# The first K tile of a decode kernel, loaded as two halves of columns from two queues

## The chip, the cores and the metric

The kernel runs on one core of one Trainium2 chip. The metric is device time in microseconds (us) of one execution. A core has five engines that each run their own program in order (TensorE, VectorE, ScalarE, GpSimd, SyncE), and 16 DMA engines that move data between the chip's main memory and the on-chip memory of 128 partitions. Programs wait for one another through semaphores; a DMA raises its semaphore when its data has landed.

## The reference

One decoding step of attention with a cache, mixed with a gated feed-forward block. Sizes: x has 448 values; there are 16 query heads and 8 K/V heads, each with a cache of 65536 positions by 256 values in bf16; the feed-forward width is 1792.

```python
g = sigmoid((x * gate_w).sum(-1))
q = (x @ wq).reshape(16 heads, 256)
scores = q . k / 16            # two query heads share one K/V head
a = softmax(scores) @ v        # reshaped to 4096 values
a = a @ wo
b = ((gate * (gate > 0)) * up) @ W_down    # gate = x @ W_gate, up = x @ W_up
out = g * a + (1 - g) * b
```

K and V together are 537 MB, the weights some 12 MB, and each byte is read once.

## The kernel before, in words

**Tiles.** Each of the 8 K/V heads has its 65536 positions cut into four tiles of 16384, for K and for V: 32 K tiles and 32 V tiles, of 8 MB each. A tile lies on 128 partitions with 128 positions (`U = 128`) of 256 values, 64 KB a partition, contiguous in main memory. Three ring buffers of that size hold all of the large data: buffer 0 first wq and W_down, then the gate and up weights, then V tiles, and wo at the end; buffers 1 and 2 hold K tiles in turn, and the last V tiles.

**What happens to a K tile.** VectorE transposes it in place in four pieces (`f_trans`, L529). TensorE then makes the scores in two halves, each of which waits for two of the four pieces (`f_qk`, L540: 64 matmuls a tile). VectorE takes the maximum (L703), ScalarE the exponential (L705). After the fourth tile of a head, a short chain rescales and transposes the probabilities, and TensorE multiplies them with the head's V tiles (`f_pv`, L584).

**The order of the work** is written out by hand. Every operation is given a key, a due time that the author reckons from a list of loads (`order`) with a price for each; an engine's program is its operations sorted by that key, and the waits follow from the declared dependencies. The loads are issued by SyncE, in this order: K0, wq (two DMAs, L626 and L627), K1, W_down (L675), K2, the gate and up weights (four DMAs, L640 and L642), K3, K4, V0, and from then on K and V in turn (L680 for K, L772 for V). A load that reuses a ring buffer waits on SyncE for the last reader of what lay there: K2 goes where K0 was and waits for K0's second half of scores; the gate and up weights wait for the q matmuls; V0 waits for the matmuls with W_down. The first four of the list wait for nothing.

**The opening.** ScalarE issues two small DMAs: x (key -9, L421) and gate_w (key -8, L422), each one row of 0.9 KB. In VectorE's program stand, in this order: constants; then what needs x (L478 and L479, then L488 to L494, with a small TensorE step at L485 between them, which turns x into columns); then what needs both x and gate_w (L464, L465; ScalarE's exponential at L466; L468 to L470; a small matmul at L471; L472, L475), which gives g and 1 - g; and then the four transposes of K0. TensorE makes q when wq is there (L501, 28 matmuls). After the transposes of K0 VectorE turns q (L632, which waits for ScalarE's copy of q, L630) and spreads it (L513); ScalarE copies the first head's part (L634); a small transpose at L635; then the scores of K0.

The load of a K tile and its transposes are declared so:

```python
kd = dma("sp", t, "r%d" % sl, lambda e, n=n, sl=sl: e.dma_start(ring[sl][:], k_src(n)), free(("k", n)))
tk = max(tL["k", n], last.get("free", 0))
tr = [op("dv", tk + 4.5 * w, f_trans(sl, w), [kd]) for w in range(4)]
```

`dma("sp", t, ...)` puts the DMA into SyncE's program with key `t`; `free` lists whose work must be over before the buffer is overwritten, and is empty for K0.

Of the kernel before, what the change touches and what calls it, by code (L numbers as in the profile page):

```python
# [27 lines left out]
class _Plan:  # L28
# [8 lines left out]
    def op(self, eng, key, fn, deps=(), tag=None):  # L37
        eng, cls = {"pv": ("pe", "pv"), "dx": ("dv", "dx"), "ap": ("ac", "ap")}.get(eng, (eng, eng))
        o = _Op(eng, key, fn, deps, tag=tag, cls=cls)
        self.ops.append(o)  # L40
        return o

    def dma(self, eng, key, sem, fn, deps=()):
        if sem not in self.dsem:
            self.dsem[sem] = self.es.enter_context(self.nc.semaphore("d_" + sem))
        o = _Op(eng, key, fn, deps, dma=sem)
        self.ops.append(o)
        return o
# [212 lines left out]
def bass_gated_mix__gqa_block_cached__glu_gated_reglu__decode_kernel(  # L261
# [20 lines left out]
    U = 128  # L282
# [14 lines left out]
    with es:  # L297
# [3 lines left out]
        ring = [sb("ring%d" % i, [128, U * DH], BF) for i in range(NRING)]  # L301
# [69 lines left out]
        op, dma = pl.op, pl.dma  # L371
# [23 lines left out]
        t = 3.0  # L395
# [10 lines left out]
        def place(kind, i):  # L406
            if kind == "k":
                return 1 + i % 2
            if kind == "v":
                return 1 + i % 2 if i >= NT - NTH else 0  # L410
            return {"vp": 2, "wo": 0}[kind]

        for kind, i, _ in order:
            if kind in ("k", "v") or (kind, i) in (("wo", 0), ("vp", 0)):
                r = place(kind, i)
# [101 lines left out]
        def k_src(n):  # L517
            h, t_ = divmod(n, NTH)
            return A_k_cache[0, h, :, :].rearrange("(p t u) d -> p t (u d)", t=NTH, u=U)[:, t_, :]
# [7 lines left out]
        def f_trans(sl, w):  # L527
            v = ring[sl][:, w * 8192:(w + 1) * 8192].bitcast(U32)
            return lambda e: e.transpose(v, v)  # L529
# [34 lines left out]
        def free(key):  # L564
            out_ = []
            for f in freed[key]:
                out_.append(l_[f] if isinstance(f, str) else qk[f[1], 1] if f[0] == "k" else pv[f[1]])
            return out_
# [55 lines left out]
        for kind, i, t in sorted(issue, key=lambda q: q[0] != "wq"):  # L624
# [51 lines left out]
            elif kind == "k":  # L676
                n = i
                h, t_ = divmod(n, NTH)
                sl = slot["k", n]
                kd = dma("sp", t, "r%d" % sl, lambda e, n=n, sl=sl: e.dma_start(ring[sl][:], k_src(n)), free(("k", n)))  # L680
                tk = max(tL["k", n], last.get("free", 0))
                tr = [op("dv", tk + 4.5 * w, f_trans(sl, w), [kd]) for w in range(4)]
                if n > 1:
                    tr[1].deps.append(aexp[n - 2])
                if t_ == 0:
# [82 lines left out]
            elif kind in ("v", "vp"):  # L768
                if kind == "v":
                    n, lo, hi = i, 0, U  # L770
                    sl = slot["v", n]
                    dep = dma("sp", t, "r%d" % sl, lambda e, sl=sl, n=n: e.dma_start(ring[sl][:], v_src(n)), free(("v", n)))  # L772
                else:
                    n, (lo, hi) = NT - 1, PIECES[i]
                    sl = slot["vp", 0]
# [96 lines left out]
```

## Time and profile before

| | |
|---|---|
| median of 3 runs | 1276.91 us (1276.64 to 1276.96) |
| the profiled execution | 1276.31 us |
| its span in the profile | 1274.5 us |
| busy: TensorE, VectorE, ScalarE | 355.0, 630.1, 77.9 us |
| moved by DMA | 549.13 MB, mean 431 GB/s |

The profiled execution's time is the metric of that one execution; the span is what lies between the first and last event of the profile, 1.8 us less. In the profile SP is SyncE, ACT ScalarE, DVE VectorE, PE TensorE (PEld its weight loads) and POOL GpSimd; SPq and ACTq are the DMA issues in the programs of SyncE and ScalarE. DMA queue q1 carries what SyncE issues, q10 what ScalarE issues; q8 and q14 fetch instructions. A row of the timeline gives the start, the duration, the engine and line, the operation with its output and input, and, in square brackets, how long the engine was idle before it and what ended that. K0, K1, ... are the K tiles in order, V0, V1, ... the V tiles.

### The profile page before, as it was taken

What the parts mean: (1) busy time and instruction counts of PE and PEld (TensorE: products, weight loads), DVE (VectorE), ACT (ScalarE), POOL (GpSimd) and SP (SyncE); (2) the same over time, 40 slices, a digit from 0 to 9 for tenths busy, and PEclk for the clock granted to TensorE, in tenths of its full rate; (3) what the DMA queues carried; (4) which work ended last, traced back from release to release, by engine and by line L of the source; (5) the groups of instructions that cost most, each with busy time, mean ns of one, the idle gap of its engine ahead of it and who ended that gap; (6) DMA issues with size and microseconds to landing.
All of it is one profiled execution on the core that took longest, in us unless ns stands there. A gap on an engine that the chain in (4) does not pass through costs nothing.

```text
span 1274.5 us, 10236 instructions
## 1 busy us (share of the span) xinstructions
PE 355.0 (28%) x4497; PEld 146.9 (12%) x4505; DVE 630.1 (49%) x309; ACT 77.9 (6%) x163; POOL 4.6 (0%) x23
## 2 busy tenths in 40 slices
PE   0534321132320332212223221323202242103524
PEld 0101110011110111101111110111100111001201
DVE  4777655553455633557433565336554355554300
ACT  0001100010000100001000010001000010000100
POOL 1000000000000000000000000000000000000000
PEclk9766665666655666656666656666566666566667
DMA  9999999999999999999999999999999999999998
GB/s 411 440 428 428 430 432 434 444 430 430 430 432 438 438 432 432 428 434 438 438 430 432 428 434 440 436 432 430 430 432 442 436 430 430 432 430 444 434 417 367
DMA packets 11389, 549.13 MB, mean 431 GB/s; under 512 B 1267, under 2 KB 1654, under 8 KB 2294
## 3 DMA queue, kind: packets, MB, share of 16 engines
q1 hardware_dynamic: 11378, 549.03, 99.7%
q8 instruction: 4, 0.07, 0.0%
q14 instruction: 3, 0.02, 0.0%
q10 hardware_dynamic: 4, 0.00, 0.0%
HBM read 549.03 MB, written 0.00 MB: 431 GB/s over the span
## 4 chain that ended last, share of the span: by engine, by line
DMA 81%; PE 15%; DVE 2%; ACT 1%; issue 1%; SPq 0%; ACTq 0%
DMA ring<-in_A_v_cache_dram 74%; PE O L584 13%; DMA ring<-in_A_wo_dram 3%; DMA ring<-in_A_wq_dram 2%; DMA ring<-in_A_k_cache_dram 2%; DVE ring L529 1%; PE ST L540 1%; ACT pcur L591 1%; PE O L501 1%; PE A_ps L551 0%; SPq L785 0%; PE O L653 0%; SPq L776 0%; DVE ring L660 0%; PE A_ps L653 0%
## 5 line engine op out<-in xcount | busy, mean ns | idle before, releaser
L529 DVE STREAM_TRANSPOSE ring<-ring 128x4096 uint32<-128x4096 uint32 x128 | 557.6, 4413 | 205.9 <-DMA ring<-in_A_k_cache_dram 205.9
L584 PE MATMUL O<-ring,pcur 128*4 128x512 bf16 x2048 | 179.6, 527 | 798.0 <-ACT pcur L591 789.4
L703 DVE TENSOR_REDUCE nmb<-ST 128x1 f32<-128x512 f32 x32 | 22.1, 692 | 336.6 <-PE ST L540 336.6
L584 PEld LDWEIGHTS O<-ring,pcur 128*4 128x4 bf16 x2048 | 57.3, 108 | 916.9 <-ACT pcur L591 802.1
L540 PE MATMUL ST<-ring,xcur 128*16 128x512 bf16 x2048 | 135.0, 416 | 45.5 <-DVE ring L529 44.9
L540 PEld LDWEIGHTS ST<-ring,xcur 128*16 128x16 bf16 x2048 | 61.0, 92 | 113.0 <-DVE ring L529 49.3
L705 ACT ACTIVATE P_sb<-ST,nmb 128x512 bf16<-128x512 f32 x32 | 44.5, 1392 | 360.3 <-DVE nmb L703 360.3
L591 ACT COPY pcur<-ptp 128x256 bf16<-128x256 bf16 x32 | 13.2, 414 | 740.4 <-DMA ring<-in_A_v_cache_dram 740.4
L607 DVE TENSOR_SCALAR o_sb<-O,rcm 128x256 bf16<-128x256 f32 x8 | 3.8, 479 | 60.9 <-PE O L584 60.9
L730 DVE TENSOR_TENSOR P_sb<-P_sb,hs 128x1024 bf16<-128x1024 bf16 x16 | 18.9, 1222 | 8.1 <-ACT hs L724 8.1
L735 PE MATMUL PT<-identb,P_sb 128*128 128x128 bf16 x128 | 13.8, 272 | 18.0 <-DVE P_sb L730 17.9
L501 PE MATMUL O<-ring,P_sb 128*128 128x512 bf16 x28 | 8.7, 484 | 17.4 <-DMA ring<-in_A_wq_dram 17.4
L735 PEld LDWEIGHTS PT<-identb,P_sb 128*128 128x128 bf16 x128 | 10.0, 121 | 20.3 <-DVE P_sb L730 20.3
L744 ACT COPY ptp<-PT 128x256 bf16<-128x256 bf16 x32 | 10.3, 375 | 22.7 <-PE PT L735 22.7
L705 ACT ACTIVATION_READ_ACCUMULATOR P_sb<-ST,nmb 128x1 f32 x32 | 8.3, 259 | 0.0
L501 PEld LDWEIGHTS O<-ring,P_sb 128*128 128x128 bf16 x28 | 3.2, 118 | 22.4 <-issue 20.8
L756 DVE RECIPROCAL rc<-M_ps 128x2 f32<-128x2 f32 x8 | 1.4, 171 | 7.5 <-PE M_ps L755 7.5
L719 PE MATMUL M_ps<-identf,hs 128*2 128x128 f32 x8 | 2.3, 283 | 10.0 <-DVE hs L717 10.0
L551 PE MATMUL A_ps<-ring,attnA 128*1 128x224 bf16 x64 | 4.1, 258 | 2.3 <-DMA ring<-in_A_wo_dram 2.2
L755 PE MATMUL M_ps<-hs,ones_f 128*128 128x2 f32 x16 | 4.5, 352 | 0.0
L557 PE MATMUL A_ps<-o_sb,ecur 128*128 128x32 bf16 x64 | 3.2, 191 | 3.1 <-DVE o_sb L610 3.1
L722 PE MATMUL M_ps<-mx,nselT 2*128 2x1 f32 x16 | 3.2, 268 | 3.0 <-DVE mx L721 3.0
(93 smaller groups left out, 69.4 us busy)
## 6 DMA issues: line engine op xcount, KB each, us to landing
ring<-in_A_v_cache_dram SPq DMA_DIRECT2D x1, 4096.0 KB, 21.9
ring<-in_A_wq_dram SPq DMA_DIRECT2D x1, 3072.0 KB, 28.9
ring<-in_A_v_cache_dram SPq DMA_DIRECT2D x1, 3072.0 KB, 28.9
ring<-in_B_W_down_dram SPq DMA_DIRECT2D x1, 1568.0 KB, 53.1
ring<-in_B_W_gate_dram SPq DMA_DIRECT2D x1, 1344.0 KB, 27.3
ring<-in_B_W_up_dram SPq DMA_DIRECT2D x1, 1344.0 KB, 30.2
ring<-in_A_wo_dram SPq DMA_DIRECT2D x1, 1232.0 KB, 33.3
ring<-in_A_v_cache_dram SPq DMA_DIRECT2D x1, 1024.0 KB, 30.9
```

What stands on the lines that cost most here:

```text
L501: ins = e.matmul(QN_ps, xw3[:, kt, 31 - m:159 - m], rhs, start=(kt == 0 and m == 0), stop=(kt == R3 and m == J // 4 - 1))
L529: return lambda e: e.transpose(v, v)
L540: ins = e.matmul(bank[32 * w:32 * w + 16, :], xcur[:, x0:x0 + 16], ktv[sl][:, u0:u0 + 16, c, :, r_], start=(b == 0 and c == 0 and r_ == 0) ...
L551: ins = e.matmul(A_ps[32 * g:32 * g + 1, 0:D2], lhsT, rhs[:, g * D2:(g + 1) * D2], start=start, stop=stop, skip_group_check=True, tile_pos ...
L584: ins = e.matmul(OP[32 * g:32 * g + 4, :], pcur[a % 2][:, 4 * k:4 * k + 4], ring[sl][:, k * 512:(k + 1) * 512], start=False, stop=False, s ...
L591: pc[n] = op("ap", max(tp - 5, last["tev", h] - 0.5), lambda e: e.copy(pcur[a % 2][:].rearrange("p (k i) -> p k i", i=4), ptp[:].rearrange ...
L703: smax[n] = op("dv", sx, lambda e, n=n, t_=t_: e.tensor_reduce(NM[:, t_:t_ + 1], ST[n % 2][:], AX.X, ALU.max, negate=True), [qk[n, 1], las ...
L705: aexp[n] = op("ac", sx + 1, lambda e, n=n, t_=t_: e.activation(P_sb[:, t_:2048:4], ST[n % 2][:], ACTF.Exp, bias=NM[:, t_:t_ + 1], scale=1 ...
L730: rsc = op("dv", tt, lambda e, pb=pb: e.tensor_tensor(pb, pb, X[:, 12:16].unsqueeze(1).to_broadcast([128, 256, 4]), ALU.mult), [h7, aexp[n]])
L735: ins = e.transpose(PT[rd][:, s * 128:(s + 1) * 128], P_sb[:, (rd * 8 + s) * 128:(rd * 8 + s + 1) * 128], identb[:, :])
L744: ins = e.copy(dst, src)
L755: l3 = mop("pe", T + 19, lambda e: e.matmul(LS_ps, ones_f[:, :], X[:, 6:8], start=True, stop=True), [l2, c_one], tag="l3")
```

## The change

K0 is loaded by two DMAs. SyncE's DMA, at its old place, now loads the first half of each partition's columns (positions 0 to 63 of its 128, 32 KB). ScalarE issues a DMA for the second half, with the key -10, which places it ahead of its x and gate_w loads. This DMA has a semaphore of its own (`k0`). All four transposes of K0 wait for both DMAs. The other K tiles are loaded as before, in one DMA each.

```diff
-                kd = dma("sp", t, "r%d" % sl, lambda e, n=n, sl=sl: e.dma_start(ring[sl][:], k_src(n)), free(("k", n)))
+                cols = slice(0, U * 128 if n == 0 else U * 256)
+                kd = dma("sp", t, "r%d" % sl, lambda e, n=n, sl=sl, cols=cols: e.dma_start(
+                    ring[sl][:, cols], k_src(n)[:, cols]), free(("k", n)))
+                kds = [kd]
+                if n == 0:
+                    kds.append(dma("ac", -10, "k0", lambda e, sl=sl: e.dma_start(ring[sl][:, U * 128:], k_src(0)[:, U * 128:])))
                 tk = max(tL["k", n], last.get("free", 0))
-                tr = [op("dv", tk + 4.5 * w, f_trans(sl, w), [kd]) for w in range(4)]
+                tr = [op("dv", tk + 4.5 * w, f_trans(sl, w), kds) for w in range(4)]
```

## The prediction

> **What bounds the kernel now.** I read the page first (the slices, the DMA queues, the chain that ended last), then the timeline and the chain in order of time for the first 105 us, then windows on the DMA. From the page:
>
> ```profile
> span 1274.5 us, 10236 instructions
> ...
> DMA  9999999999999999999999999999999999999998
> ...
> q1 hardware_dynamic: 11378, 549.03, 99.7%
> ...
> q10 hardware_dynamic: 4, 0.00, 0.0%
> ...
> DMA 81%; PE 15%; DVE 2%; ACT 1%; issue 1%; SPq 0%; ACTq 0%
> ```
>
> The 16 DMA engines are busy in every slice, with SyncE's queue (q1) on them 99.7% of the time. The time is 549 MB at their rate plus every moment in which they have nothing queued; compute matters only where it makes a load start late. So the question is not when the first K tile K0 lands, but whether SyncE's next issue still comes before its queue has drained. The opening, from the timeline (start, length; in brackets the engine's idle time before and who ended it):
>
> ```profile
> 0.71 0.53 ACTq L421 DMA_DIRECT2D P_sb<-in_A_x_dram  x1
> 0.72 0.41 SPq L680 DMA_DIRECT2D ring<-in_A_k_cache_dram  x1
> ...
> 1.28 0.21 ACTq L422 DMA_DIRECT2D scr<-in_gate_w_dram  x1
> ...
> 4.91 0.18 DVE L478 COPY scr<-P_sb 1x64 bf16<-1x64 bf16 x1
> ...
> 6.04 0.18 DVE L494 COPY P_sb<-xT 128x4 bf16<-128x4 bf16 x1
> ...
> 10.08 0.61 DVE L464 TENSOR_TENSOR ptp<-P_sb,scr 1x448 f32<-1x448 bf16 x1 [3.86 <-DMA scr<-in_gate_w_dram]
> ...
> 14.32 0.23 DVE L475 TENSOR_SCALAR mg<-emat,gb 128x4 f32<-128x4 bf16 x1
> 22.78 17.42 DVE L529 STREAM_TRANSPOSE ring<-ring 128x4096 uint32<-128x4096 uint32 x4 [8.23 <-DMA ring<-in_A_k_cache_dram]
> ...
> 31.45 8.68 PE L501 MATMUL O<-ring,P_sb 128*128 128x512 bf16 x28 [17.36 <-DMA ring<-in_A_wq_dram]
> ...
> 40.84 0.45 DVE L632 STREAM_TRANSPOSE scr<-ptp 128x256 uint32<-128x256 uint32 x1 [0.64 <-ACT ptp L630]
> ...
> 44.35 4.96 PE L540 MATMUL ST<-ring,xcur 128*16 128x512 bf16 x64 [0.65 <-issue]
> ...
> 49.36 0.33 SPq L680 DMA_DIRECT2D ring<-in_A_k_cache_dram  x1
> ```
>
> To be seen: ScalarE's two 0.9 KB loads (x, gate_w) land before K0. VectorE goes through the x and gate work (L478 to L475, done at 14.55), idles 8.23 us for K0, transposes it until 40.20, turns q, and TensorE's scores of K0 (44.35 on) free the ring buffer for the third K tile K2, issued at 49.36. That issue is the first that waits for compute.
>
> **How the queues share an engine.** A packet's bytes are counted at its start (columns: stretch, length, busy time of five engines, granted clock, DMA share, GB/s):
>
> ```profile
> 1.60:2.40 0.80, 0.00 (x0) 0.00 (x0) 0.62 (x5) 0.00 (x0) 0.64 (x3) 1.00 3.87 1312
> 2.40:4.60 2.20, 0.00 (x0) 0.00 (x0) 1.84 (x7) 0.00 (x0) 1.59 (x9) 1.00 0.00 0
> 4.60:5.60 1.00, 0.27 (x5) 0.22 (x5) 0.54 (x4) 0.00 (x0) 0.67 (x5) 1.00 2.42 1049
> ...
> 7.00:8.00 1.00, 0.00 (x0) 0.00 (x0) 0.00 (x0) 0.00 (x0) 0.00 (x0) 1.00 2.42 1049
> ...
> 9.40:10.40 1.00, 0.00 (x0) 0.00 (x0) 0.32 (x1) 0.00 (x0) 0.00 (x0) 1.00 2.42 1049
> ```
>
> 1049 GB/s over 1 us is 16 packets of 64 KB: every engine starts one K0 packet (one partition) each 2.42 us. gate_w, issued at 1.28, ended VectorE's wait at 10.08, just as the fourth burst began. q10 shows four packets for two loads, so each is data and a completion. The reading that fits: on an engine the two queues take turns packet by packet, and each of gate_w's two packets let 64 KB of K0 pass (one more was already under way).
>
> **The change, part by part.**
>
> *Removed and added issues.* SyncE's issue keeps its 0.41 us. ScalarE gets one of about that length (row at 0.72) ahead of its two, which move from 0.71 and 1.28 to about 1.2 and 1.7. ScalarE's next work waits for the gate_w chain: no cost in itself.
>
> *K0's arrival.* Both halves go over the same 16 engines. Packets become 32 KB and take turns, 8 and 8 per engine. At the same rate K0 is complete where it was, 22.7. Every transpose waits for both halves, so none starts earlier. Two queues could at best lift this stretch from 422 GB/s to the page's best slice, 444:
>
> ```profile
> 1.70:21.60 19.90, 0.85 (x7) 0.71 (x7) 5.55 (x23) 1.49 (x2) 3.62 (x17) 1.00 1.01 422
> 21.60:30.00 8.40, 0.00 (x0) 0.00 (x0) 7.22 (x2) 0.00 (x0) 0.00 (x0) 1.00 0.98 418
> ```
>
> 19.9 x (1 - 422/444) = 1.0 us; I take 0 (the packets run back to back already), with 1.0 as the other end.
>
> *x and gate_w, moved behind 4 MB.* They are now last in ScalarE's own queue, in order behind K0's second half. On the engine that carried gate_w, packets of 2.42 us put K0's end, landing included, at 10.08 + 5 x 2.42 = 22.2. Then come x's data, its completion, gate_w's data and its completion, each taking turns with a packet of wq (3072 KB in 128 packets, so 24.6 thousand bytes; from the 418 GB/s row above at share 0.98, 24.6 x 16 x 0.98 / 418 = 0.92 us).
>
> ```profile
> ring<-in_A_wq_dram SPq DMA_DIRECT2D x1, 3072.0 KB, 28.9
> ```
>
> Three or four of these: gate_w lands at 24.9 or 25.9; I take the middle, **25.4**. Lower end 22.8 (with K0), upper end in the rivals.
>
> *VectorE's order.* Queued behind the two waits, on an engine that works in order, are the gate chain and K0's four transposes. From gate_w's landing to the end of L475 it was 14.55 - 10.08 = 4.5 us (a ScalarE exponential with its table load and a small matmul among it), formerly inside the 8.23 us of idle. That cover is now gone: the transposes start at 25.4 + 4.5 = 29.9 instead of 22.78 and end at 47.35 instead of 40.20. The q matmuls need x only at 31.45 (x lands two turns earlier, its own chain takes 6.2 - 4.9 = 1.3 us), so they end at 40.1 as before, and the copy at L630 that L632 waited for, 0.64 us, now hides behind the transposes: L632 starts at 47.4 against 40.84, **+6.5 us**.
>
> *Scores of K0.* From L632 to K2's issue were 49.36 - 40.84 = 8.52 us, of which 4.99 the 64 matmuls. They ran half at each clock:
>
> ```profile
> 44.40:46.70 2.30, 2.30 (x24) 0.79 (x28) 0.00 (x0) 0.00 (x0) 0.00 (x0) 0.50 1.05 456
> 46.75:49.20 2.45, 2.45 (x44) 1.08 (x36) 0.00 (x0) 0.00 (x0) 0.00 (x0) 1.00 1.02 435
> ```
>
> and a half of a later tile's scores, from the timeline, all of it at 0.50:
>
> ```profile
> 84.09 3.59 PE L540 MATMUL ST<-ring,xcur 128*16 128x512 bf16 x32 [10.89 <-DVE ring L529]
> ```
>
> All at half clock the 64 would take 2 x 3.59 = 7.2, all at full clock 3.6. TensorE will have been idle 10 us instead of 4, so it starts at half clock again; I take 5.4. The Trainium skill ("TensorE: Matmul & The Clock Gate", Part 1) says the activity window is free-running and of about 3.4 us, so the clock may rise up to two windows late; that agrees with a rise 2.4 us into these matmuls, and by it the term would lie between 5.4 and 7.2, the time between my forecast and 1.8 us above it. K2's issue: 49.36 + 6.5 + 0.4 = **56.3**.
>
> *When the queue drains.* K0, wq, K1 and W_down are all issued in the first microseconds. K0's time from issue to landing, on an empty queue, and K2's in the chain (start, length):
>
> ```profile
> DMA to landing us min/median/max: 22.0/22.0/22.0
> ```
>
> ```profile
> 49.36 25.87 DMA ring<-in_A_k_cache_dram
> ...
> 104.28 36.72 DMA ring<-in_A_v_cache_dram
> ```
>
> The DMA around the point where K2 takes over, and the instruction fetches between 46 and 58:
>
> ```profile
> 53.20:54.10 0.90, 0.00 (x0) 0.00 (x0) 0.90 (x1) 0.00 (x0) 0.00 (x0) 0.70 2.64 1104
> 54.10:55.40 1.30, 0.00 (x0) 0.00 (x0) 1.30 (x1) 0.00 (x0) 0.00 (x0) 0.50 0.30 120
> 55.40:56.40 1.00, 0.00 (x0) 0.00 (x0) 1.00 (x1) 0.00 (x0) 0.00 (x0) 0.50 2.12 918
> ```
>
> ```profile
> q8 instruction: 2, 0.03, 1.1%
> ```
>
> The burst from 53.2 is K2's first packets on most engines: there the old queue ends, and K2, issued 3.8 us earlier, was ready. At 56.3 + 1.1 (K0's first burst lies 0.9 to 1.7 after its issue) it is not: those engines stand idle for about 4 us, **the first hole in the DMA stream**. K2's landing was 49.36 + 25.87 = 75.2; from an empty queue it is 56.3 + 22.0 = 78.3, or +3.1. But 75.2 holds a lag that K0's 22.0 doesn't: K2's eight packets from 53.2 to 54.1 on, 19.4 us of them and 0.3 to land (K0: its eighth burst ends at 21.5 to 22.5), would be done at 72.9 to 73.8, so some engines ran 1.4 to 2.3 late, those whose K2 burst comes only at 55.4. I put that down to the instruction fetches (q8). Fetches that fall into the hole cost nothing, later ones do. Bounds: all of the lag gone, +3.1; all kept, +3.1 + 1.8 = 4.9. I take two thirds kept, **+4.3**.
>
> *What is late next.* Again from the timeline, and the load that follows K2 in the queue:
>
> ```profile
> 52.13 17.42 DVE L529 STREAM_TRANSPOSE ring<-ring 128x4096 uint32<-128x4096 uint32 x4 [2.07 <-DMA ring<-in_A_k_cache_dram]
> ...
> 73.25 0.33 SPq L680 DMA_DIRECT2D ring<-in_A_k_cache_dram  x1
> ```
>
> ```profile
> ring<-in_B_W_gate_dram SPq DMA_DIRECT2D x1, 1344.0 KB, 27.3
> ```
>
> K1's transposes start after K0's scores, near 57.0 instead of 52.13, so K3's issue moves by 4.9 to about 78. Behind K2, done near 79, lie the gate and up weights (over 2.7 MB, 6 us or more): hidden. V0 (at 104.28) takes 36.7 to land against 22.0 on an empty queue, so it has some 15 us in hand. No later hole opens, none closes, and no idle DMA time exists to absorb this one. The sum against the profiled execution (1276.31, span 1274.5): 1276.31 + 4.3 = 1280.6. The median of the runs lies 0.6 above that execution, so as a median **1281.2**.
>
> **Rivals.**
>
> *Turns of whole transfers.* If an engine finished a transfer's share before it changes queue, x would wait for wq (8 x 0.92 = 7.3 us) and gate_w also for wq's tail (512 KB, 1.3 us): gate_w at 22.2 + 8.6 = 30.8, 5.4 later than mine, **1286.6**. Against it: gate_w had landed by 10.08, in the middle of K0. The Trainium skill ("DMA: Bandwidth & Descriptors", Queues, rings and completion order) speaks for it: an engine drains a packet of typically 9 to 17 descriptors from one queue before it switches, which is one load's share here. The trace disagrees, by that 10.08. 8%.
>
> *ScalarE's queue first (not slower).* Should the engines serve K0's second half ahead of the first, it ends near 12 and gate_w near 14; the 4.5 us chain fits in the idle time before 22.78, nothing moves: **1276.9**. It decides at a landing of about 21.7: then K2's issue is 2.8 us later, at 52.2, and its packets just meet the queue's end at 53.3. For it: x, issued 0.01 us before K0, was served at once. Against it: gate_w was made to wait 8.8 us. 9%.
>
> *Starved.* If ScalarE's half waited for SyncE's backlog, it would land near 52, K2's issue would be some 33 us late: about **1307**. The four q10 packets, served in the midst of q1, speak against it. 2%.
>
> *A better rate.* Two queues at 444 GB/s save 1.0 us and the 4.3 shrink to 3.3: **1280.2**, still slower; no mechanism in the trace takes off 2.6 us.
>
> **How the numbers follow.** Measurement can tell about 0.2%, 2.6 us: faster is below 1274.4, slower above 1279.5. The forecast has 79% (the better rate in it); its own range adds the ends (gate_w 24.9 to 25.9, scores 4.6 to 6.5, lag none to all): 1278.5 to 1283.5, and some 6 of the 79 lie under 1279.5. Transfers whole 8%, ScalarE first 9%, starved 2%; 2% is left for a gain that I see no mechanism for. Faster 2%, same 9 + 6 = 15%, slower 83%. All ends of the terms at once, scores at 3.6 and 7.2 among them, give 1277.7 to 1284.1; toward the whole transfers I go to 1285.5. Range: 1277.7 to 1285.5.
>
> **What would show it.** Right: VectorE's idle ahead of L478 or L464 ends after 23; the first L529 starts near 30, not 22.8; L632 near 47.4 follows it with no wait for ScalarE; K2's issue near 56; DMA share near 0 around 54 to 57; K2 to landing 22 to 24 us instead of 25.9. Wrong: gate_w landing before 21.7 (no hole), at 30 (whole transfers), or a hole that a later stretch gives back.

## The result, and the profile after

The changed kernel takes **1280.62 us** (median of 6 runs, 1279.55 to 1282.21) against 1276.64 for the kernel before in the same measurement (1276.15 to 1276.96). The ratio is 1.0034, 95% interval 1.0023 to 1.0045: 4.0 us slower. The forecast was 1281.2. The profiled execution is the fastest of the six, 1279.55, with a span of 1277.8, 3.3 us longer than before.

From the page of the kernel before, the GB/s of the 40 slices:

```profile
GB/s 411 440 428 428 430 432 434 444 430 430 430 432 438 438 432 432 428 434 438 438 430 432 428 434 440 436 432 430 430 432 442 436 430 430 432 430 444 434 417 367
```

From the page of the changed kernel, the span, the same row and two queues:

```profile
span 1277.8 us, 10238 instructions
...
GB/s 410 380 433 447 431 427 431 433 441 433 429 431 439 435 435 429 429 443 433 433 429 429 447 433 429 429 431 445 433 429 429 431 445 433 429 429 433 443 419 365
...
q1 hardware_dynamic: 11378, 544.84, 98.7%
q10 hardware_dynamic: 148, 4.20, 0.8%
```

The loss begins in one slice: the second (32 to 64 us) moves 380 GB/s, where the page of before had 440. 60 GB/s over 32 us are 1.9 MB, 4.4 us of DMA time, which is more than the 3.3 us by which the span grew: bytes are counted at the start of a packet, and the third and fourth slice, 433 and 447 against 428 and 428, make up for part of it. Over the first twelve slices together the changed kernel is 43 GB/s short, some 3.2 us, and over all forty 41. q10 now holds 148 packets: 128 of K0's second half, 16 completions, and the four small ones.

The opening of the changed kernel, from its timeline:

```profile
0.71 0.39 ACTq L685 DMA_DIRECT2D ring<-in_A_k_cache_dram  x1
0.72 0.41 SPq L681 DMA_DIRECT2D ring<-in_A_k_cache_dram  x1
...
1.71 0.24 ACTq L422 DMA_DIRECT2D scr<-in_gate_w_dram  x1
...
23.23 0.19 DVE L478 COPY scr<-P_sb 1x64 bf16<-1x64 bf16 x1 [18.22 <-DMA P_sb<-in_A_x_dram]
...
25.09 0.61 DVE L464 TENSOR_TENSOR ptp<-P_sb,scr 1x448 f32<-1x448 bf16 x1 [0.49 <-DMA scr<-in_gate_w_dram]
...
29.34 0.23 DVE L475 TENSOR_SCALAR mg<-emat,gb 128x4 f32<-128x4 bf16 x1
29.47 17.41 DVE L529 STREAM_TRANSPOSE ring<-ring 128x4096 uint32<-128x4096 uint32 x4
...
46.81 0.40 DVE L632 STREAM_TRANSPOSE scr<-ptp 128x256 uint32<-128x256 uint32 x1
...
50.28 4.99 PE L540 MATMUL ST<-ring,xcur 128*16 128x512 bf16 x64 [0.65 <-issue]
55.31 0.33 SPq L681 DMA_DIRECT2D ring<-in_A_k_cache_dram  x1
```

Both halves are issued within 0.01 us of each other. VectorE's 8.23 us of idle for K0 has turned into 18.22 us of idle for x; the transposes follow L475 with no bracket, that is, with no wait for K0 at all. They start 6.7 us later than before, and K2 is issued 5.95 us later. From the chain that ended last, and from windows on the DMA around K2's issue (columns: stretch, length, busy time of five engines, granted clock, DMA share, GB/s):

```profile
55.31 23.16 DMA ring<-in_A_k_cache_dram
```

```profile
53.20:54.10 0.90, 0.90 (x20) 0.51 (x16) 0.00 (x0) 0.00 (x0) 0.00 (x0) 1.00 0.27 97
54.10:56.20 2.10, 1.17 (x22) 0.40 (x12) 0.88 (x2) 0.16 (x1) 0.00 (x0) 1.00 0.00 0
56.20:57.20 1.00, 0.00 (x0) 0.00 (x0) 1.00 (x1) 1.00 (x2) 0.00 (x0) 1.00 3.09 1049
```

Here is the hole: from 54.1 to 56.2 no DMA engine starts a packet, and 0.9 to 1.9 us after K2's issue all 16 start together (1049 GB/s over 1 us). The trace also holds the start and the duration of every packet. Added up, they leave the 16 engines idle for 2.75 us on average between 52 and 60 us, and for 0.00 us from 60 to 1200; in the kernel before they are 0.00 in both. K2 lands at 55.31 + 23.16 = 78.47 against 75.23 before, +3.24, and the execution's time is 3.24 longer.

### The profile page after: what moved, and what is told of

The parts are those of the page before. It is cut to its first block, busy times and chain, and to the rows that moved or that the text cites. A ratio compares the mean times of both kernels' runs of the same rounds, so it can differ in the third digit from the quotient of the medians.

```text
span 1277.8 us, 10238 instructions
## 1 busy us (share of the span) xinstructions
PE 362.5 (28%) x4497; PEld 152.0 (12%) x4505; DVE 630.0 (49%) x309; ACT 78.0 (6%) x163; POOL 4.6 (0%) x23
## 4 chain that ended last, share of the span: by engine, by line
DMA 80%; PE 15%; DVE 2%; issue 1%; ACT 1%; SPq 0%; ACTq 0%
DMA ring<-in_A_v_cache_dram 73%; PE O L584 13%; DMA ring<-in_A_wo_dram 3%; DMA ring<-in_A_wq_dram 2%; DMA ring<-in_A_k_cache_dram 2%; DVE ring L529 1%; PE ST L540 1%; ACT pcur L591 1%; PE O L501 1%; PE A_ps L551 0%; SPq L790 0%; PE O L653 0%; SPq L781 0%; DVE ring L660 0%; PE A_ps L653 0%
## 5 line engine op out<-in xcount | busy, mean ns | idle before, releaser
L584 PE MATMUL O<-ring,pcur 128*4 128x512 bf16 x2048 | 185.9, 541 | 791.6 <-ACT pcur L591 783.3
L708 DVE TENSOR_REDUCE nmb<-ST 128x1 f32<-128x512 f32 x32 | 22.1, 691 | 343.2 <-PE ST L540 343.2
## 6 DMA issues: line engine op xcount, KB each, us to landing
ring<-in_A_k_cache_dram ACTq DMA_DIRECT2D x1, 4096.0 KB, 22.1
ring<-in_A_k_cache_dram SPq DMA_DIRECT2D x1, 4096.0 KB, 22.3
ring<-in_A_v_cache_dram SPq DMA_DIRECT2D x1, 4096.0 KB, 22.2
```

The costliest lines, as they stand in the source:

```text
L584: ins = e.matmul(OP[32 * g:32 * g + 4, :], pcur[a % 2][:, 4 * k:4 * k + 4], ring[sl][:, k * 512:(k + 1) * 512], start=False, stop=False, s ...
L708: smax[n] = op("dv", sx, lambda e, n=n, t_=t_: e.tensor_reduce(NM[:, t_:t_ + 1], ST[n % 2][:], AX.X, ALU.max, negate=True), [qk[n, 1], las ...
```

## The experiments

Times are medians. The kernel before took 1276.48 beside the first four kernels, 1276.32 beside the next four and 1276.27 beside the single executions that came last. The theory: x and gate_w, queued behind 4 MB on ScalarE's queue, hold up VectorE's program; K2 is issued after the DMA queue has drained; the hole is lost. Its main rival: the split itself costs (two queues, smaller packets, a second wait).

**1. x and gate_w ahead of the second half.**

```diff
-                    kds.append(dma("ac", -10, "k0", ...
+                    kds.append(dma("ac", -7, "k0", ...
```

> K0 is still loaded in two halves from two queues, but ScalarE issues x and gate_w first and K0's second half third. Theory (the late gate chain holds up K0's transposes, so that K2 is issued after the DMA queue has drained): gate_w lands before 8, VectorE is done with L475 before K0 is there, K0 lands at 22.7 to 24.5 (its second half now starts behind a packet or two of the first), K2 is issued at 49.4 to 51, before the queue drains near 53.3, and the time is that of before, 1276.6 (within 0.7). Rival (two queues, half-sized packets or the second wait cost by themselves): the 4.0 us stay, 1280.6.

Measured: 1276.46, ratio 1.0001 (0.9992 to 1.0010). The split is still there and the loss is gone: the rival falls. The way there was not as expected. From a second profiled execution of this kernel, its timeline:

> The kernel with x and gate_w issued first, one more look: its first profile was of its slowest run (1278.6, median 1276.46), with K0 landing at 25.9 and K2 issued at 53.0 after scores of 6.3 us. Theory: in a typical run K0 lands as late, near 25.9, the scores take about 5 us, K2 is issued near 51.7, just before the queue drains, and the time is 1276.2 to 1277.3. Rival: K2's issue is again near 53 and the time still 1276.5, which would mean that the hole isn't what costs.

```profile
7.56 0.61 DVE L464 TENSOR_TENSOR ptp<-P_sb,scr 1x448 f32<-1x448 bf16 x1 [1.33 <-DMA scr<-in_gate_w_dram]
...
25.83 17.42 DVE L529 STREAM_TRANSPOSE ring<-ring 128x4096 uint32<-128x4096 uint32 x4 [13.80 <-DMA ring<-in_A_k_cache_dram]
...
46.64 5.10 PE L540 MATMUL ST<-ring,xcur 128*16 128x512 bf16 x64 [0.65 <-issue]
51.78 0.33 SPq L681 DMA_DIRECT2D ring<-in_A_k_cache_dram  x1
```

gate_w is early, but K0 is there only at 25.8, 3 us later than in one piece. K2 is issued 2.4 us later than before, and the time (1276.29) doesn't move: lateness as such costs nothing. In the first profiled execution, of 1278.60 and the longest of its runs, K2 was issued at 53.04, and there it did cost. The edge lies between.

**2. No split, but x and gate_w late.** SyncE loads K0 whole, as the first of its program; ScalarE's x load waits for it.

```diff
-        d_x = dma("ac", -9, "x", lambda e: e.dma_start(x_row, A_x[0, :, :]))
+        k0d = dma("sp", -20, "r%d" % slot["k", 0], lambda e: e.dma_start(ring[slot["k", 0]][:], k0_src))
+        d_x = dma("ac", -9, "x", lambda e: e.dma_start(x_row, A_x[0, :, :]), [k0d])
...
-                kd = dma("sp", t, "r%d" % sl, ...
+                kd = k0d if n == 0 else dma("sp", t, "r%d" % sl, ...
```

> No split at all: K0 is one load by SyncE as before, but ScalarE issues x only when K0 has landed, and gate_w behind it. Theory: x is issued at 22.8, the two small loads then take turns with packets of wq of 0.9 us, gate_w lands at 27 to 29 against 25.07 in the changed kernel, K0's transposes start 4.4 us after that, K2's issue comes 2 to 4 us later than the 55.3 of the changed kernel, and the time is 1282.5 to 1284.5. Rival (the split costs by itself): no split, no loss, 1276.6.

Measured: 1284.74, ratio 1.0064 (1.0050 to 1.0078), a little above the expected range. From its chain: gate_w, from issue to landing.

```profile
0.72 21.90 DMA ring<-in_A_k_cache_dram
...
23.20 6.17 DMA scr<-in_gate_w_dram
```

gate_w lands at 29.4, K2 is issued at 60.83. Without any split the loss is twice that of the change: late small loads are enough.

**3. Both halves on SyncE.**

```diff
-                    kds.append(dma("ac", -10, "k0", ...
+                    kds.append(dma("sp", t + 0.001, "k0", ...
```

> Both halves of K0 are issued by SyncE, one behind the other; ScalarE issues x and gate_w alone as in the kernel before. Theory: gate_w lands near 6 to 10, nothing is late, 1276.6 (within 0.5). Rival (32 KB packets and the second semaphore cost by themselves): 1280.6, or part of it.

Measured: 1276.24, ratio 0.9999 (0.9990 to 1.0008). K2 was issued at 49.54, against 49.36 before. The 32 KB packets and the second semaphore cost nothing that shows.

**4. Two more small loads between x and gate_w.**

```diff
+        pads = [dma("ac", -8.5 + 0.1 * i_, "pad%d" % i_, lambda e, i_=i_: e.dma_start(
+            scr[0:1, 704 + 128 * i_:832 + 128 * i_], A_x[0, :, 0:128])) for i_ in range(2)]
         d_gw = dma("ac", -8, ...
-        z0 = op(..., [d_x, d_gw])
+        z0 = op(..., [d_x, d_gw] + pads)
```

> The changed kernel with two more small loads (256 bytes each, not used) that ScalarE issues between x and gate_w. Theory (on a DMA engine the two queues take turns packet by packet, and each small load is a data packet and a completion): two loads are four turns with wq packets of 0.9 us, so gate_w lands 3.7 us later, at 28.7, K2 is issued at 59 and the time is 1284.3. If a whole transfer's share went before each turn, gate_w would land after all of wq and much of K1, beyond 31, and the time would be over 1287; if small loads waited for nothing, 1280.6.

Measured: 1284.14, ratio 1.0064 (1.0050 to 1.0078). From its timeline (L466 is L464 of the other kernels):

```profile
28.73 0.61 DVE L466 TENSOR_TENSOR ptp<-P_sb,scr 1x448 f32<-1x448 bf16 x1 [4.30 <-DMA scr<-in_gate_w_dram]
33.10 17.42 DVE L531 STREAM_TRANSPOSE ring<-ring 128x4096 uint32<-128x4096 uint32 x4
...
59.15 0.33 SPq L683 DMA_DIRECT2D ring<-in_A_k_cache_dram  x1
```

gate_w at 28.7 and K2's issue at 59.15 are the forecast values, 3.6 and 3.8 us behind the changed kernel. Small loads queued behind a large one go out in turns, two each, 0.9 us a turn here.

**5. Gate weights ahead of K2.** The DMA queue gets 3.7 us more to do while K0's scores are late.

```diff
+                tg_ = (54.0, t)
...
-                    a1.append(dma("sp", t + 0.01 * i_, "r0", ...
+                    a1.append(dma("sp", tg_[i_] + 0.01 * i_, "r0", ...
```

(the same for the second DMA of each weight)

> The changed kernel, but SyncE issues the two gate weight loads (1568 KB, 3.7 us of DMA) ahead of K2 instead of behind it; they wait only for the q matmuls, over at 40. gate_w and K0's transposes are as late as in the changed kernel. Theory (only the hole in the DMA stream costs, not the lateness): the queue drains near 57 instead of 53.3, K2 issued at 55.3 is in time, no hole there; K2 then lands near 78.9, and K4, which waits for K2's scores, is issued near 100, just when K3 ends, so a hole of up to 1.5 us can open there: 1276.6 to 1278.1. Rival (each microsecond by which K0's transposes are late is lost): 1280.6.

Measured: 1279.75, ratio 1.0024 (1.0015 to 1.0034): neither 1276.6 to 1278.1 nor 1280.6. The profiled execution was the longest of its runs, 1282.20. A second one:

> The kernel with the gate weights ahead of K2, one more look: its first profile was of its slowest run (1282.2, median 1279.75). Theory: in a typical run there is again no hole at K2, K2 lands at 79 to 80 instead of 82.0, K4 is issued near 100.5 to 101.5 and the hole lies there, with the time 1278.5 to 1280.7. Rival (no hole at K4 either, the time is lost by the lateness itself): K4 is issued before 98.5 and the time is still over 1279.

That execution took 1278.42. Its windows, its timeline and its chain:

```profile
54.10:56.20 2.10, 1.05 (x20) 0.33 (x12) 1.00 (x2) 0.27 (x1) 0.00 (x0) 1.00 1.02 426
...
99.00:100.60 1.60, 1.60 (x20) 0.54 (x16) 0.00 (x0) 0.00 (x0) 0.00 (x0) 0.51 0.66 287
```

```profile
100.89 0.33 SPq L682 DMA_DIRECT2D ring<-in_A_k_cache_dram  x1
```

```profile
55.20 24.70 DMA ring<-in_A_k_cache_dram
```

At K2 the hole is gone: 426 GB/s where the changed kernel had 0, though K2 is issued as late as there. But K2 now lies behind more work, lands at 79.9, and K4, which waits for K2's scores, is issued at 100.89; in the longest run K2 landed at 82.04 and K4 was issued at 103.18. The 287 GB/s from 99.0 to 100.6 prove little by themselves, since bytes are counted at the start of a packet; the changed kernel shows less there:

```profile
99.00:100.60 1.60, 1.60 (x24) 0.59 (x20) 0.69 (x1) 0.26 (x1) 0.00 (x0) 0.52 0.28 123
```

The starts and durations of the packets decide: between 98 and 108 us the engines idle 0.80 us on average in this execution and 3.55 in the longest run, against 0.00 in the changed kernel. The hole has moved to the next place where a load waits for compute. I had allowed 1.5 us of loss in all; it was 2.1 in this execution (1278.42 against 1276.27), 1.0 of it idle engines, and 3.3 over the runs. What the other 1.1 us are is open, so this run shows that a filler that is wanted early shifts the hole, but not that the hole is the whole loss.

**6. TensorE kept warm.** Forty matmuls of zeros into the score bank of K1, which K1's scores overwrite, ahead of K0's scores.

```diff
+                l_["warm"] = op("pv", tq + 9.68, f_warm, [l_["qn"], c_ze, g_idb, c_ps[1]])
```

> The changed kernel with 40 extra matmuls of a zero vector on TensorE between the q matmuls and K0's scores, into the score bank of K1, which K1's scores overwrite: they do nothing but keep TensorE's clock up. Theory: K0's 64 score matmuls take 3.6 us at full clock instead of 5.0, K2 is issued 1.4 us earlier (53.9 against 55.3), the hole shrinks by as much: 1279.2; and the spread of the runs (1279.55 to 1282.21 in the changed kernel), which I put down to the clock's rise falling at a different place in each run, shrinks to under 1 us. Rival (the spread comes from the DMA queues' turns): 1279.2 but the spread stays at 2 us or more.

> The changed kernel once more, on the chip of the three others of this call: 1280.6 (within 1), with a spread of 2 us or more between its runs against under 1 us for the kernel before, if the length of K0's scores varies with the clock and nothing hides it.

Measured on one chip: warm 1280.06 (1278.25 to 1281.59), the changed kernel 1281.08 (1279.67 to 1282.08). From the warm kernel's timeline:

```profile
50.14 3.86 PE L540 MATMUL ST<-ring,xcur 128*16 128x512 bf16 x64 [0.72 <-issue]
54.06 0.33 SPq L686 DMA_DIRECT2D ring<-in_A_k_cache_dram  x1
```

The scores take 3.86 instead of 4.99 us and K2 is issued 1.25 us earlier. TensorE's granted clock was 1.00 throughout these 3.86 us, and 0.50 in the first 2.4 of the 4.99. The medians differ by 1.0, which is not clear of the spread of the runs. That spread is no smaller (3.3 us against 2.4), so the theory of the spread falls. The kernel before spread over 1.4 us in 12 runs, where under 1 was expected. Two more executions:

> The changed kernel, one more look, for the spread of its runs. So far the profiled executions with a hole follow time = K2's issue + 1224.1 us (1223.9 to 1224.7). Theory (all that varies lies before K2's issue): this look keeps to that sum within 0.6, wherever in 1279.5 to 1282.2 it falls. Rival (what varies is how far single DMA engines lag after the hole, from instruction fetches): the time moves by 1 us or more with K2's issue at 55 to 56 as before.

> The kernel with TensorE kept warm, one more look: its runs spread as widely (1278.25 to 1281.59) as without, so the clock during K0's scores isn't what varies. Theory and rival as for the look at the changed kernel: the sum K2's issue + 1224.1 holds within 0.6, or K2's issue stays near 54 and the time moves.

The changed kernel's took 1281.29, from its timeline:

```profile
50.06 6.28 PE L540 MATMUL ST<-ring,xcur 128*16 128x512 bf16 x64 [0.65 <-issue]
56.40 0.33 SPq L681 DMA_DIRECT2D ring<-in_A_k_cache_dram  x1
```

In three profiled executions of the changed kernel K0's scores took 4.99, 5.51 and 6.28 us, and the times were 1279.55, 1279.67 and 1281.29; in the last the granted clock stayed at 0.50 for some 5 us of the scores. So part of the spread is the clock. The sum was off by 0.8 in that execution, outside the 0.6 I gave, and 0.6 of it lies between K2's issue and its landing, 23.75 us instead of 23.16. The warm kernel's second execution took 1278.36 with scores of 3.93 us and keeps to the sum, but its runs without a profile went up to 1281.59; what moves those stays open.

**7. The gate chain behind K0's transposes.**

```diff
-        z0 = op("dx", 1, ...
+        z0 = op("dx", 36.5, ...
```

(and z1 to z9, the rest of L465 to L475, with keys from 36.6 to 40.96)

> The changed kernel with all its loads, but what needs gate_w (L464 to L475) stands behind K0's transposes in VectorE's program, and its ScalarE and TensorE steps behind the copy of q; what needs x stays in front. Theory: the transposes wait only for x (23.2) and its 1.4 us chain, start at 24.6 instead of 29.5 and end at 42.0; L464 and L465 (1.3 us) and the copy of q (0.6) now stand between them and L632, and 0.6 us of matmul ahead of K0's scores; K2 is issued near 53.1, 2.2 us earlier than in the changed kernel: 1278.4 (within 0.8). Rival (the split costs by itself): 1280.6.

Measured: 1280.44, ratio 1.0032 (1.0021 to 1.0043), against 1281.08 for the changed kernel on that chip; expected was 1278.4. From its timeline:

```profile
24.30 17.43 DVE L529 STREAM_TRANSPOSE ring<-ring 128x4096 uint32<-128x4096 uint32 x4
...
42.96 1.28 ACT L630 ACT_TABLE_LOAD   x1 [42.96 <-DVE gz L465]
44.26 0.59 ACT L630 CAST ptp<-O 128x512 bf16<-128x512 f32 x1
...
44.87 0.45 DVE L632 STREAM_TRANSPOSE scr<-ptp 128x256 uint32<-128x256 uint32 x1 [2.02 <-ACT ptp L630]
...
54.35 0.33 SPq L681 DMA_DIRECT2D ring<-in_A_k_cache_dram  x1
```

The transposes start 5.2 us earlier, as expected, but most of it is lost again: the chain's work now stands between them and the scores, with a table load of 1.28 us ahead of the copy of q, which I hadn't counted. K2's issue moves by 1.0 us instead of 2.2, and the profiled execution by 0.5 (1279.03). The medians are too close to tell the two kernels apart, so the case is weak by itself; it fits the table below.

**All of it in one table.** K2's issue, its landing, the idle time of the DMA engines and the time of the same profiled execution, for all kernels but the one with the gate weights first. The idle time is the mean of the 16 engines between 45 and 130 us, from the starts and durations of the packets.

| execution | K2 issued | K2 landed | engines idle | time |
|---|---|---|---|---|
| before | 49.36 | 75.23 | 0.00 | 1276.31 |
| both halves on SyncE | 49.54 | 75.17 | 0.00 | 1276.24 |
| small loads first, second execution | 51.78 | 75.23 | 0.00 | 1276.29 |
| small loads first, first execution | 53.04 | 77.45 | 0.69 | 1278.60 |
| warm, first execution | 54.06 | 76.83 | 1.68 | 1278.25 |
| warm, second execution | 54.29 | 77.30 | 2.03 | 1278.36 |
| chain behind | 54.35 | 77.92 | 1.91 | 1279.03 |
| changed kernel, first execution | 55.31 | 78.47 | 2.75 | 1279.55 |
| changed kernel, second execution | 55.64 | 78.20 | 3.13 | 1279.67 |
| changed kernel, third execution | 56.40 | 80.15 | 4.07 | 1281.29 |
| two more small loads | 59.15 | 81.1 | 6.81 | 1283.17 |
| no split, small loads late | 60.83 | 83.1 | 8.52 | 1284.74 |

Up to 51.8 no engine idles and the time doesn't move; from 54.06 to 60.83 the issue is 6.77 us later and the time 6.49 longer. So K2's issue, whatever makes it late, sets most of the loss. It doesn't set all of it: the execution with the issue at 53.04 idled only 0.69 us and lost 2.3, more than the two warm ones, whose issue came a microsecond later. Its K2 took 24.41 us from issue to landing, theirs 22.8 and 23.0. From K2's landing to the end it is 1201.1 to 1201.5 us in the first ten rows, and 1202.1 and 1201.6 in the last two, so the rest of the differences arises mostly between K2's issue and its landing, which with a hole took 21.9 to 24.4 us. No version beat the kernel before by more than the intervals.

## Why the prediction was right, step by step

- *K0's arrival* unchanged, and no gain from two queues: right. SyncE's half landed 22.3 us after its issue and ScalarE's 22.1, against 22.0 for the whole.
- *gate_w at 25.4*: by 25.09, which fits three turns (24.9) and not four (25.9). Turns packet by packet, as read from gate_w's 8.8 us of before; the rival of whole transfers (30.8) and that of ScalarE's queue first fall with this row.
- *The chain of 4.5 us with its cover gone*: 29.47 for the transposes against 29.9. L632 at 46.81 with no wait for ScalarE, +5.97 against +6.5.
- *Scores 5.4 us*: 4.99 in this execution, 5.51 and 6.28 in others. K2's issue 55.31 against 56.3.
- *The hole and the lag*: the engines idled 2.75 us on average, where about 4 was forecast. K2's 23.16 from issue to landing are 22.0 and 1.16 of lag, where two thirds of 1.8 were taken. That this share came so close is luck: over the executions with a hole in the table K2 took from 21.9 to 24.4 us. +3.24 for this execution against +4.3: the 1.0 us lies in K2's issue, 0.6 of it ahead of L632 and 0.4 in the scores. That the lag comes from instruction fetches was argued and not tried. The packets of this execution bear it out: followed from end to start on each engine, one engine carries a 16 KB instruction fetch of 0.95 us between two packets of K2, and it ends K2 1.0 us after the last of the other fifteen. No run left the fetches out, and this wasn't settled for the others.
- *What is late next*: K3's issue moved from 73.25 to 76.93 and V0's from 104.28 to 107.20, and neither opened a hole (0.00 us idle behind 60 us).
- Over all runs the loss was 4.0 us against 4.3. That the median came so close is luck in part: the profiled execution was forecast 1.0 us too slow (1280.6 against 1279.55), and the median lies 1.1 us above it, not 0.6. Some of that can be the length of the scores, hidden before, which now counts; but the warm kernel, with short scores, has its median 1.8 us above its profiled execution, so it can't be all.

## What to carry to other kernels

In a kernel bound by DMA, look for the first load that waits for compute and for the time at which the queue ahead of it runs dry: work before that load is free up to that point and costs roughly one for one behind it. A large load at the head of an engine's queue holds up every small one that this engine issues behind it: two 0.9 KB loads behind 4 MB cost 4 us here, and with the two ahead of it the same split cost nothing. Splitting a transfer over two queues didn't bring it in sooner, since one queue already kept the DMA engines full.

## What the runs showed that I had not expected

- With x and gate_w first, ScalarE's half of K0 took 24.2 us to land and SyncE's 19.5; in equal turns from the start they took 22.1 and 22.3. A second half that starts a few turns later finishes several packets of the next transfer later, 3 us here.
- gate_w issued into a busy queue, behind an x that was issued 0.55 us before it, took 6.17 us to land (experiment 2), as long as 6.7 turns of 0.92 us; queued behind the large load from the start, x and gate_w together were there 2.9 us after K0's reckoned end at 22.2, some three turns.
- The same 64 matmuls took from 3.86 to 6.29 us, by how much of them ran before the granted clock rose.
